# Reordering the head of a fused state-space and gated-MLP kernel: first gate blocks behind two x tiles, weights in fewer and later pieces

## The chip, the cores and the metric

The kernel runs on one core of one Trainium2 chip. The metric is the device time of one execution in microseconds (us); lower is better. The engines are TensorE (PE in the profile, its weight loads PEld), VectorE (DVE), ScalarE (ACT), GpSimd (POOL) and SyncE (SP, which here only issues transfers). Transfers are issued on three queues: SP's, ScalarE's and, for three tiny ones, POOL's.

## The reference

Input x is 2048 tokens of 448 features. It is normalised, goes through a diagonal complex recurrence (448 states) and, beside it, through a gated MLP of width 1792; both are combined:

```python
xn = _layernorm(x, axis=-1)
# A: Lam_bar = exp(dt*Lam);  h_t = Lam_bar*h_{t-1} + B_bar x_t
#    s = 2*Re(C h) + xn*Dskip
s = _A_ref(xn, ...)
# B: g = xn@w_gate; u = xn@w_up; h = sigmoid(g)*u; h@w_down
g = _silu(_B_ref(xn, w_gate, w_up, w_down))
return x + s * g
```

All inputs and the output are bf16.

## The kernel before

The tokens are worked in four chunks of 512 (`NC_`, index c), each of four tiles of 128 tokens (`TPC`). For a chunk the normalised, transposed x stands in `xnT[c % 3]`, in 7 slabs of 64 features, doubled over the two halves of the partitions. The hidden width 1792 is worked in 14 blocks of 128 columns. A *step* `gu_mm(c, k, m, ...)` computes, for k = "g" (gate) or "u" (up), column tile m of both halves of the width: 7 pairs of matmuls (L707, L708), one in each half of the array, into the two banks of a PSUM pair `gu[a]` (three pairs, used in turn by `next_gu`). A gate step is evacuated by ScalarE (Tanh, L721), an up step by VectorE (L724). I write g0.m and u0.m for chunk 0. There are 7 gate and 7 up steps; in chunk 0 the gates come first. Then comes `b_phase` (the state's input matrix), the scans on VectorE, the down projection and the output, chunk by chunk. Two more PSUM banks `acc` serve the transposes and the down projection.

The program is written as operations with costs, reads and writes (`Plan.add`). TensorE runs them in the order written, and while `pl.seq` is set so does VectorE. `Plan.solve` gives each a due time by going back from TensorE's order, then simulates, and each engine's instructions are emitted in the order of the simulated starts. Transfers have a cost of issue and a `rate` in bytes per microsecond that tells the plan when they land; `slot` is the plan's number of a transfer, of which it lets eight be under way at once. The real queues take an eighth-next transfer only when the semaphore that it shares has told of the earlier landing. The rate is a plan's figure only: it can change the order of the instructions, not what a transfer does.

The head, before the first full step, is what the change touches:

- *Loads* (L351 to L412). `load_x` brings tiles of x (112 KB each), `load_w` a block of columns of `w_gate` or `w_up` for one half of the partitions, cut by `BLK`: gate in column tiles (0,2), (2,4), (4,7), 224, 224 and 336 KB a half; up in (0,3), (3,7), 336 and 448 KB a half. SP issues x0, gate half 0 in three, then up in both halves' first blocks, x4 to x7 as one, and up's second blocks, then `dbc`, then the transposing loads of `bT` and all that follows. ScalarE issues x1, x2 and x3 as one, and gate half 1 in three. POOL issues the three rows `vrow`.
- *Norm of tiles 0 to 3*. `stats(t)` (VectorE, L424, L425), `chain(t, 1)` (square root on ScalarE L450, copy on POOL L451, reciprocal on VectorE L452), `norm(t)` (VectorE L469), `pe_transpose(t)` (TensorE L501 to L503), copy to `xnT` (ScalarE for tile 0, L506; VectorE for the others, L509).
- *Columns* (L535). Five tiny matmuls turn `vrow` into columns in a bank of a `gu` pair; VectorE copies them to `pv` (L546); POOL works out `dt`, `theta`, `turn` (L554 to L560), which ScalarE's L575 needs for the tables of sine and cosine.
- *`silu_table`* (L568) loads ScalarE's second table, ahead of all Tanh.

The order of the head stands in L962 to L989: statistics of tiles 0 and 1 and their norms, statistics of tiles 2 and 3, transposes of 0 and 1, columns, norms of 2 and 3, then

```python
    for j in range(2):
        for m in range(2):
            gu_mm(0, "g", m, slots0[m], j, j + 1, not (j or m))
    pe_transpose(2)
    pe_transpose(3)
    silu_table()
    pl.seq = False
    gu_mm(0, "g", 2, slots0[2], 0, 2, True)
    for m in range(3):
        gu_mm(0, "g", m, slots0[m], 2, 4, False)
        gu_evac(0, "g", m, slots0[m])
```

where j counts tiles of 128 tokens: the first blocks are 128 tokens wide, then come four of 256, then g0.3 on with all 512. Tiles 4 to 7 are normed by `stats_for(1)` and `prepare(1)`, ScalarE doing the norm (L474) and SP transposing loads (L375).

## Time and profile before

| what | us |
|---|---|
| runs (median; lowest; highest; three runs) | 185.26; 185.0; 186.19 |
| profiled execution: span from first to last instruction | 183.7 |
| first gate matmul / first matmul of w_up / first of `b_phase` | 7.89 / 19.91 / 30.6 |
| busy: TensorE / VectorE / ScalarE / GpSimd | 177.4 / 166.4 / 94.8 / 34.2 |

Of the profiled execution the record keeps the span and no other time; the span lies 1.6 us under the median of the runs. A line of the timeline has start, busy time, engine, source line, operation, output and inputs, the count and, in brackets, the idle time before it and what ended it. A line of the waits has who waited for whom, the sum, the number of times and the longest. A line of the stretches has each engine's busy time with its number of instructions, then the granted clock, the share of time in which DMA engines were busy (over 1 where packets overlap) and GB/s. The page's rows of digits cut the span into 40 slices, each digit the busy share in tenths.

### The profile page before, as it was taken

To read this page: it belongs to the slowest core of one execution; us is meant where nothing else is said; L and a number is where in the kernel's file an instruction comes from. 1 tells how busy PE (TensorE), PEld (TensorE's weight loads), DVE (VectorE), ACT (ScalarE), POOL (GpSimd) and SP (SyncE) were. 2 spreads that over 40 slices of the span, in tenths; PEclk is the share of its full clock that TensorE was granted. 3 is DMA by queue.
4 is the path that set the end of the run, shared out by engine and by line. 5 is a ranking of instruction groups with operands and counts; after the bars stand their busy time and mean duration, and the time that the engine had idled before them with its cause. 6 is when DMAs were issued, how large, how long until landed. Compare 5 with 4: busy or idle time off the path is not lost.

```text
span 183.7 us, 3601 instructions
## 1 busy us (share of the span) xinstructions
PE 177.4 (97%) x1402; PEld 90.4 (49%) x1402; DVE 166.4 (91%) x296; ACT 94.8 (52%) x152; POOL 34.2 (19%) x95
## 2 busy tenths in 40 slices
PE   7699999999999999999999999999999999999992
PEld 2585555465554444455554444444555444455551
DVE  3873899899999998999999999999999998999973
ACT  3689993958599978665310452367120445211100
POOL 7370465000048557700000000000000000000000
PEclk9999999999999999999999999999999999999999
DMA  5999994489801370243000000002000000001121
GB/s 137 255 225 223 155 166 90 90 256 266 231 0 26 74 82 21 50 82 71 0 2 0 29 0 0 4 0 75 0 4 0 25 25 5 25 0 52 57 73 50
DMA packets 30258, 13.44 MB, mean 73 GB/s; under 512 B 19744, under 2 KB 30240, under 8 KB 30240
## 3 DMA queue, kind: packets, MB, share of 16 engines
q1 hardware_dynamic: 28336, 12.05, 30.7%
q10 hardware_dynamic: 1808, 1.15, 2.5%
q8 instruction: 11, 0.18, 0.4%
q14 instruction: 7, 0.06, 0.1%
q0 software_dynamic: 96, 0.00, 0.0%
HBM read 6.77 MB, written 1.84 MB: 47 GB/s over the span
## 4 chain that ended last, share of the span: by engine, by line
PE 93%; DMA 3%; DVE 1%; issue 1%; POOL 1%; DVEq 0%; POOLq 0%
PE gu L707 45%; PE gu L903 14%; PE acc L932 11%; PE acc L903 9%; PE gu L775 8%; DMA hF<-in_A_Lambda_re_dram 3%; PE gu L708 2%; PE acc L778 2%; PE gu L761 2%; POOL hF L353 1%; PE acc L501 0%; DVE o_t L948 0%; PE acc L764 0%; DVE o_t L944 0%; DVE o_t L941 0%
## 5 line engine op out<-in xcount | busy, mean ns | idle before, releaser
L708 PE MATMUL gu<-xnT,wG 64*128 64x512 bf16 (+2 forms) x245 | 46.0, 333 | 0.0
L707 PE MATMUL gu<-xnT,wG 64*128 64x512 bf16 (+2 forms) x245 | 46.0, 333 | 0.0
L707 PE MATMUL gu<-xnT,wU 64*128 64x512 bf16 x196 | 45.8, 376 | 0.0
L708 PE MATMUL gu<-xnT,wU 64*128 64x512 bf16 x196 | 45.8, 376 | 0.0
L721 ACT ACTIVATE sig<-gu 128x1024 f32<-128x1024 f32 x21 | 21.3, 1021 | 22.0 <-PE gu L708 21.9
L903 PEld LDWEIGHTS <-hF 128*128 128x128 bf16 x224 | 21.9, 98 | 20.7 <-issue 0.2
L707 PEld LDWEIGHTS <-wG 64*128 64x128 bf16 x245 | 21.9, 94 | 18.7
L707 PEld LDWEIGHTS <-wU 64*128 64x128 bf16 x196 | 18.4, 94 | 22.1
L724 DVE SCALAR_TENSOR_TENSOR hF<-sig,gu 128x1024 bf16<-128x1024 f32 x21 | 25.5, 1216 | 2.9 <-PE gu L708 1.6
L903 PE MATMUL gu<-wd,hF 128*128 128x448 bf16 x140 | 27.9, 352 | 0.0
L842 DVE TENSOR_TENSOR_SCAN wv<-c_r,st,z 128x512 bf16<-128x512 f32 x18 | 22.9, 1276 | 0.0
L932 PE MATMUL acc<-cT,hT 128*128 128x448 bf16 (+1 forms) x112 | 22.6, 346 | 0.0
L708 PEld LDWEIGHTS <-wG 64*128 64x128 bf16 x245 | 21.8, 94 | 0.0
L909 ACT ACTIVATE g_t<-gu 128x448 bf16<-128x448 f32 x10 | 5.4, 541 | 29.2 <-DVE o_t L946 12.9
L708 PEld LDWEIGHTS <-wU 64*128 64x128 bf16 x196 | 18.4, 94 | 0.0
L789 ACT CAST bus<-gu 128x1024 bf16<-128x1024 f32 x12 | 11.9, 1011 | 12.4 <-PE gu L761 12.2
L903 PE MATMUL acc<-wd,hF 128*128 128x448 bf16 x84 | 16.9, 352 | 0.0
L775 PE MATMUL gu<-xnT,bT 128*128 128x512 bf16 x72 | 16.7, 379 | 0.0
L932 PEld LDWEIGHTS <-hT 128*128 128x128 bf16 x119 | 11.5, 98 | 10.1 <-issue 0.4
L424 DVE BATCH_NORM_STATS2 bst<-x_all 128x6 f32<-128x448 bf16 x12 | 7.0, 610 | 5.7 <-DMA x_all<-in_A_x_dram 5.7
L795 ACT CAST bus<-acc 64x256 bf16<-64x256 f32 (+1 forms) x24 | 8.8, 369 | 6.4 <-PE acc L778 6.1
L944 DVE TENSOR_TENSOR o_t<-acc,xd 128x448 bf16<-128x448 f32 (+1 forms) x16 | 9.6, 601 | 1.3 <-PE acc L932 1.2
(138 smaller groups left out, 240.1 us busy)
## 6 DMA issues: line engine op xcount, KB each, us to landing
out_dram<-o_t SPq DMA_DIRECT2D x15, 112.0 KB, 1.7
wd<-in_B_w_down_dram SPq DMA_DIRECT2D x2, 784.0 KB, 5.5
x_all<-in_A_x_dram SPq DMA_DIRECT2D x3, 448.0 KB, 4.5
wU<-in_B_w_up_dram SPq DMA_DIRECT2D x2, 448.0 KB, 12.2
wU<-in_B_w_up_dram SPq DMA_DIRECT2D x2, 336.0 KB, 7.6
wG<-in_B_w_gate_dram SPq DMA_DIRECT2D x2, 224.0 KB, 6.5
wG<-in_B_w_gate_dram ACTq DMA_DIRECT2D x2, 224.0 KB, 6.6
xnT<-xn SPq DMA_TRANSPOSE x24, 2.4
```

The lines of the kernel that those rows point to most:

```text
L424: add("DVE", 0.6, lambda: V.bn_stats(out=bst[b][:], in_=x_all[:, t, :]), r=[("x", t)], w=[("bst", b)])
L707: T.matmul(gu[a][:, 0, ts], lhsT=w_[0:H, s, ms], rhs=x[0:H, s, ts], start=(s == 0), stop=(s == 6))
L708: T.matmul(gu[a][:, 1, ts], lhsT=w_[H:P, (s + 1) % 7, ms], rhs=x[H:P, s, ts], start=(s == 0), stop=(s == 6))
L721: add("ACT", act(1024), lambda: A.activation(th, gu[a][:], ACT.Tanh, scale=0.5), r=[("gu", a)], w=[tk])
L724: add("DVE", dve1(1024), lambda: V.scalar_tensor_tensor(out=ho, in0=th, scalar=1.0, in1=gu[a][:], op0=ALU.add, op1=ALU.mult), r=[("gu", a) ...
L775: T.matmul(gu[slots[pt]][:, i, :], lhsT=bT[:, kt, i, pt * P:pt * P + P], rhs=x[:, 2 * kt, :], start=(first and kt == 0), stop=(not first a ...
L789: add("ACT", act(1024), lambda: A.copy(out=bus[u][:], in_=gu[slots[pt]][:]), r=key(pt), w=[("bus", u)])
L795: add("ACT", 0.3, lambda ns=ns, d=d, q=q, l=l, i=i: A.copy(out=bus[u][d, l, ns], in_=acc[a3[i]][q, 0:256]), r=[("acc", a3[i])] + ([("bus", ...
L842: dve(1.194, lambda k=k: V.tensor_tensor_scan(out=wv[:, k, :], data0=rb, data1=z[:, k, :], initial=(st[pt][:, k, :] if c else 0.0), op0=AL ...
L903: T.matmul(d, lhsT=hF[c % 2][:, m, h, js], rhs=wd[:, ft, :], start=(ft == 0), stop=(ft == FT - 1))
L932: T.matmul(y, lhsT=hT[c % 2][:, hm, js], rhs=cT[:, cm, c0:c1], start=(i == 0 and not on_pe), stop=(i == 6))
L944: add("DVE", dve1(n), lambda od=od, y=y, c0=c0, c1=c1: V.tensor_tensor(out=od, in0=y, in1=xq[:, c0:c1], op=ALU.add), r=[key, ("xd", q)], w ...
```

## The change

Loads: x tiles 2 and 3 become two transfers, one on each queue, each behind the first gate block of its queue. x4 to x7 goes ahead of the third gate block on SP. The third gate block of half 1 is issued by ScalarE behind the copy of tile 0's transposes. `w_up` is loaded in one transfer for each half (784 KB): half 0 by SP behind the gate blocks, half 1 by ScalarE, written behind the square root of tile 3. Some rates and slots of the plan differ.

Order: TensorE runs g0.0 and g0.1 on tile 0 and 1, a step at a time, right behind the two tiles' transposes; then tile 2's transposes, g0.2 on tiles 0 and 1, tile 3's transposes, the columns, and then the three steps on tile 2 and on tile 3, 128 tokens at a time. g0.3 has all 512 tokens and goes to the two `acc` banks, from which two Tanh of 512 columns take it. VectorE copies tile 1's transposes before the statistics of tile 2, which with its norm come before those of tile 3; statistics of tile 4 come before tile 3's copy. ScalarE takes over the copy of tile 2's transposes and that of the columns. The columns use an `acc` bank.

In the built program ScalarE's instructions then stand in this order: square roots 0 and 1, copy 0, issue of the third gate block (waits for the landing of half 1's first gate block), square roots 2 and 3, copy 2, table load, columns, issue of `w_up` (waits for the landing of SP's third gate block), Tanh of g0.0, g0.1, g0.2, then Tanh of g0.4, g0.5, g0.6 with norms of tiles 4 to 7 and the four L575 among them, then the Tanh of g0.3. On SP `dbc` and `bT` follow half 0 of `w_up`.

```diff
-    BLK = {"g": [(0, 2), (2, 4), (4, 7)], "u": [(0, 3), (3, 7)]}
+    BLK = {"g": [(0, 2), (2, 4), (4, 7)], "u": [(0, 7)]}
...
     load_x(0, 1, "SP")
+    load_x(1, 1, "ACT")
     load_w("SP", "g", 0, 0, rate=90e3)
-    load_w("SP", "g", 0, 1)
-    load_x(1, 1, "ACT")
-    load_x(2, 2, "ACT")
     load_w("ACT", "g", 1, 0, rate=90e3)
-    load_w("SP", "g", 0, 2)
-    load_w("ACT", "g", 1, 1)
-    load_w("ACT", "g", 1, 2)
+    load_x(2, 1, "SP", rate=300e3)
+    load_x(3, 1, "ACT", rate=300e3)
+    load_w("SP", "g", 0, 1, rate=165e3)
+    load_w("ACT", "g", 1, 1, rate=165e3)
+    load_x(4, 4, rate=230e3)
+    load_w("SP", "g", 0, 2, rate=150e3)
...
-    for h in range(2):
-        load_w("SP", "u", h, 0, rate=215e3)
-    load_x(4, 4, rate=140e3)
-    for h in range(2):
-        load_w("SP", "u", h, 1, rate=260e3)
+    load_w("SP", "u", 0, 0, rate=150e3, slot=10)
...
-        add("DVE", 0.6, lambda: V.bn_stats(out=bst[b][:], in_=x_all[:, t, :]), r=[("x", t)], w=[("bst", b)])
+        add("DVE", 0.6, lambda: V.bn_stats(out=bst[b][:], in_=x_all[:, t, :]),
+            r=[("x", t)] + ([("xnT", 0, 3, "a")] if 4 < t < 8 else []), w=[("bst", b)])
...
-        if t == 0:
+        if t in (0, 2):
             add("ACT", 0.85, lambda: A.copy(out=xnT[0][:, :, js], in_=tp[:, :, :]),
...
-        vps = flat(gu[a][:, 0, 0:12], 4, 3)
+        vps = flat(acc[a][:, 0:12], 4, 3)
...
-        add("DVE", 0.1, lambda: V.tensor_copy(out=pv[:].rearrange("p k i -> p i k"), in_=vps[:]), r=[("gu", a)], w=["pv"])
+        add("ACT", 0.2, lambda: A.copy(out=pv[:].rearrange("p k i -> p i k"), in_=vps[:]), r=[("acc", a)], w=["pv"])
...
+        if a is None:
+            for i in range(2):
+                add("ACT", act(512), lambda i=i: A.activation(th[:, i, :], acc[i][:], ACT.Tanh, scale=0.5),
+                    r=[("acc", i)], w=[tk] if i == 0 else [(tk, 1)])
...
-    stats(2)
-    stats(3)
     slots0 = [next_gu() for _ in range(3)]
     pe_transpose(0)
+    load_w("ACT", "g", 1, 2, rate=150e3, r=[("xnT", 0, 0, "a")], slot=11)
     pe_transpose(1)
-    columns(slots0[2])
-    for t in (2, 3):
-        chain(t, 1)
-        norm(t)
-    for j in range(2):
-        for m in range(2):
+    stats(2)
+    chain(2, 1)
+    norm(2)
+    stats(3)
+    chain(3, 1)
+    load_w("ACT", "u", 1, 0, rate=150e3, r=[("sd", 3)], slot=13)
+    norm(3)
+    for m in range(2):
+        for j in range(2):
             gu_mm(0, "g", m, slots0[m], j, j + 1, not (j or m))
     pe_transpose(2)
+    stats(4)
+    for j in range(2):
+        gu_mm(0, "g", 2, slots0[2], j, j + 1, not j)
     pe_transpose(3)
+    columns(0)
     silu_table()
     pl.seq = False
-    gu_mm(0, "g", 2, slots0[2], 0, 2, True)
-    for m in range(3):
-        gu_mm(0, "g", m, slots0[m], 2, 4, False)
-        gu_evac(0, "g", m, slots0[m])
+    for j in range(2, 4):
+        for m in range(3):
+            gu_mm(0, "g", m, slots0[m], j, j + 1, False)
+            if j == 3:
+                gu_evac(0, "g", m, slots0[m])
+    gu_mm(0, "g", 3, None, 0, TPC, False)
+    gu_evac(0, "g", 3, None)
...
-    for i in range(3, 13):
+    for i in range(4, 13):
         gu_step(0, i)
```

More of the change, by code (lines that the diff above doesn't have):

```diff
@@ L358, in load_x, with load_w @@
              x_all[:, t0:t0 + n, :], x_src[:, t0:t0 + n, :], r=r, rate=rate)
-    BLK = {"g": [(0, 2), (2, 4), (4, 7)], "u": [(0, 3), (3, 7)]}
-    def load_w(eng, k, half, b, r=(), rate=105e3):
+    BLK = {"g": [(0, 2), (2, 4), (4, 7)], "u": [(0, 7)]}
+    def load_w(eng, k, half, b, r=(), rate=105e3, slot=None):
         m0, m1 = BLK[k][b]
@@ L368, in load_w @@
              wsrc[k][:, c0 + m0 * P:c0 + m1 * P].rearrange("(s p) f -> p s f", p=H), cost=0.65, r=r, rate=rate)
+        if slot is not None:
+            pl.ops[-1].slot = slot
     def load_wd(h):
@@ L542, in f @@
                 T.matmul(vps[h * H:h * H + H, 3, :], lhsT=vrow[:, 384:448], rhs=ident[0:3, 0:3], start=True, stop=True)
-        add("PE", 0.4, f, r=["ident"] + [("vrow", k) for k in range(3)], w=[("gu", a)])
+        add("PE", 0.4, f, r=["ident"] + [("vrow", k) for k in range(3)], w=[("acc", a)])
         pv = sbt("pv", [3, 4], FP32)
         dt_b = C("dt", 4, BF16)
-        add("DVE", 0.1, lambda: V.tensor_copy(out=pv[:].rearrange("p k i -> p i k"), in_=vps[:]), r=[("gu", a)], w=["pv"])
+        add("ACT", 0.2, lambda: A.copy(out=pv[:].rearrange("p k i -> p i k"), in_=vps[:]), r=[("acc", a)], w=["pv"])
         dt_b = C("dt", 4, BF16)
@@ L567, in silu_table @@
     def silu_table():
-        add("ACT", 1.3, lambda: A.preload_act_table_set("silu_and_others"), r=[("sd", t) for t in range(4)], w=["silutab"])
+        add("ACT", 1.3, lambda: A.preload_act_table_set("silu_and_others"), r=[("sd", t) for t in range(4)] + [("xnT", 0, 2, "a")], w=["silutab"])
     def tables():
@@ L700, in gu_mm @@
         x = xnT[c % 3]
+        bank, keys = ([gu[a][:, 0, :], gu[a][:, 1, :]], [("gu", a)]) if a is not None else (
+            [acc[0][:], acc[1][:]], [("acc", 0), ("acc", 1)])
         ts = slice(lo * P, hi * P)
@@ L706, in f @@
             for s in range(7):
-                T.matmul(gu[a][:, 0, ts], lhsT=w_[0:H, s, ms], rhs=x[0:H, s, ts], start=(s == 0), stop=(s == 6))
-                T.matmul(gu[a][:, 1, ts], lhsT=w_[H:P, (s + 1) % 7, ms], rhs=x[H:P, s, ts],
+                T.matmul(bank[0][:, ts], lhsT=w_[0:H, s, ms], rhs=x[0:H, s, ts], start=(s == 0), stop=(s == 6))
+                T.matmul(bank[1][:, ts], lhsT=w_[H:P, (s + 1) % 7, ms], rhs=x[H:P, s, ts],
                          start=(s == 0), stop=(s == 6))
@@ L711, in gu_mm @@
         return add("PE", 7 * (0.0028 + n / 2400.0) + (2 * SW if first else 0), f,
-                   r=xr(c, lo, hi) + [("w", k, 0, m), ("w", k, 1, m)], w=[("gu", a)], name=f"{k}{c}.{m}")
+                   r=xr(c, lo, hi) + [("w", k, 0, m), ("w", k, 1, m)], w=keys, name=f"{k}{c}.{m}")
     sg_n = [0]
@@ L719, in gu_evac @@
         ho, hk = hF[c % 2][:, m, :, :], ("hF", c % 2, m)
-        if k == "g":
+        if a is None:
+            for i in range(2):
+                add("ACT", act(512), lambda i=i: A.activation(th[:, i, :], acc[i][:], ACT.Tanh, scale=0.5),
+                    r=[("acc", i)], w=[tk] if i == 0 else [(tk, 1)])
+        elif k == "g":
             add("ACT", act(1024), lambda: A.activation(th, gu[a][:], ACT.Tanh, scale=0.5),
@@ L725, in gu_evac @@
                                                                  op0=ALU.add, op1=ALU.mult),
-                r=[("gu", a), tk], w=[hk])
+                r=[("gu", a), tk] + ([(tk, 1)] if (tk, 1) in pl.w else []), w=[hk])
     def gu_step(c, i, first=False):
@@ L993, in stats_for @@
             if c not in (3,):
-                stats(t)
+                if t != 4:
+                    stats(t)
             elif t % 2:
```

## The prediction

> **What bounds the kernel now.** I read the page first: share of TensorE, then its row over the 40 slices; after that the timelines of the head and the loads.
>
> ```profile
> PE 177.4 (97%) x1402; PEld 90.4 (49%) x1402; DVE 166.4 (91%) x296; ACT 94.8 (52%) x152; POOL 34.2 (19%) x95
> PE   7699999999999999999999999999999999999992
> PEclk9999999999999999999999999999999999999999
> ```
>
> TensorE is busy in every slice but the first two and the last, at full clock, so the kernel is one unbroken row of matmuls between a head and a tail. Nothing after the head has slack: what the head gains or loses reaches the end unchanged. A later stall is not made up either. So the question is only: at what moment does the gapless row stand at a fixed point of it, say the first up matmul, before and after? I call that matmul u0.0.
>
> The timeline of TensorE from 5 to 20 us, cut to the rows where its work changes:
>
> ```profile
> 5.34 0.51 PE L501 MATMUL acc<-ident,xn 128*128 128x128 bf16 x6 [0.49 <-DVE xn L469]
> ...
> 7.63 0.21 PE L540 MATMUL gu<-ident,hF 3*128 3x3 bf16 x3 [0.99 <-DMA hF<-in_A_Lambda_re_dram]
> 7.89 0.23 PE L707 MATMUL gu<-xnT,wG 64*128 64x128 bf16 x1
> 9.56 0.51 PE L501 MATMUL acc<-ident,xn 128*128 128x128 bf16 x6
> 10.79 0.28 PE L707 MATMUL gu<-xnT,wG 64*128 64x256 bf16 x1
> 13.87 0.38 PE L707 MATMUL gu<-xnT,wG 64*128 64x512 bf16 x1
> 19.91 0.38 PE L707 MATMUL gu<-xnT,wU 64*128 64x512 bf16 x1
> ```
>
> The columns wait for the last of three tiny loads (0.99 us), and the first gate block stands behind them. The starts give prices: columns 0.26 us; four 128-column blocks with their lead-in 1.55 (0.39 each); a tile's transposes 0.62; eight 128-columns' worth at width 256 3.08; four full steps 6.04, so 1.51 each. From 7.63 to 19.91 there is no gap.
>
> The timeline of VectorE shows what a tile's norm costs:
>
> ```profile
> 5.46 0.40 DVE L469 TENSOR_SCALAR xn<-x_all,meanf,rsd 128x448 bf16<-128x448 bf16 x1
> 5.78 0.62 DVE L424 BATCH_NORM_STATS2 bst<-x_all 128x6 f32<-128x448 bf16 x1
> 6.43 0.18 DVE L425 BATCH_NORM_AGGREGATE mv<-bst 128x2 bf16<-128x6 f32 x1
> ...
> 7.26 0.59 DVE L509 COPY xnT<-acc 128x896 bf16<-128x896 bf16 x1
> ...
> 8.35 0.40 DVE L469 TENSOR_SCALAR xn<-x_all,meanf,rsd 128x448 bf16<-128x448 bf16 x1
> 8.92 0.40 DVE L469 TENSOR_SCALAR xn<-x_all,meanf,rsd 128x448 bf16<-128x448 bf16 x1
> ```
>
> Statistics of tiles 2 and 3 fill the pause in which VectorE would wait for the transposes of tile 1; both tiles are normed by 9.32, before TensorE asks at 9.56. That cover is what the change gives up.
>
> Last the loads: the view of the tile wU, and three stretches (5 to 11, 12 to 19, 19 to 22 us; last columns clock, DMA share, GB/s).
>
> ```profile
> L353 SPq DMA_DIRECT2D wU<-in_B_w_up_dram x4: 595/616/630, 7.1 to 9.8; - x4
> DMA to landing us min/median/max: 7.1/9.9/12.7
> 5.00:11.00 6.00, 4.67 (x97) 3.81 (x99) 4.49 (x15) 3.70 (x7) 2.69 (x11) 1.00 1.10 248
> 12.00:19.00 7.00, 7.00 (x86) 4.61 (x84) 3.37 (x8) 7.00 (x10) 1.34 (x4) 1.00 1.12 222
> 19.00:22.00 3.00, 3.00 (x31) 1.60 (x28) 2.88 (x11) 3.00 (x7) 1.18 (x3) 1.00 1.38 129
> ```
>
> The DMA engines are full until 20 us: 248 GB/s while both queues have work, 222 with SP's alone. The last part of wU lands at 9.8 + 12.7 = 22.5. Today that harms nobody: u0.0 needs only the first three column tiles of wU (336 KB a half, issued at 7.1 and 7.7, median 7.6 us to landing, so by about 16), and step 3, which needs the rest, starts at 19.91 + 3 x 1.51 = 24.4.
>
> **The change, part by part.**
>
> *Start of the first block.* It stands behind the copy of tile 0 alone (6.07 to 6.98) and its weights. x0, x1 and both first gate blocks are 672 KB, moved by about 5.0 us at the rates shown; landing follows the last byte by about 1. So it starts at 7.03 instead of 7.89: 0.86 earlier, of which 0.26 goes back where the columns now stand.
>
> *Tiles 2 and 3.* VectorE now copies tile 1 first (transposes done 6.64, copy from 6.70; such copies follow each other by 0.55) and starts tile 2's statistics at 7.25 instead of 5.78. From statistics to norm: 0.65 + 0.22 + 0.44 + 0.26 = 1.57 (rows of tile 1), norm 0.40, transposes 0.05 later: tile 2's transposes at 9.26. Tile 3's statistics follow that norm by 0.32, at 9.13; its transposes start at 9.13 + 2.02 = 11.15, against 10.18 now. TensorE has 1.55 us of work from 7.03 and idles from 8.58 to 9.26, then 0.62 + 0.78 and idles from 10.66 to 11.15.
>
> *From there to u0.0.* 11.15 + 0.62 + 0.26 (columns) + 2.33 (six 128-column blocks) + 6.04 = 20.40. Width 128 in place of 256 costs 0.002 a pair, nothing. So TensorE alone reaches u0.0 0.49 later than now.
>
> *Statistics of tile 4 ahead of the copy of tile 3.* They wait for x4..7, whose bytes (896 KB of x, 896 KB of gate blocks, part of the late one) were moved by 9.3 to 10.8 us in the run before; with 0.7 to 1.5 to landing (an estimate: ScalarE's last gate block landed at 3.15 + 9.1 = 12.2, and its bytes with all ahead of them had been moved by about 11) that is 10 to 12.3. The copy is needed at 13.16, so landing up to 11.7 is free: 0 to 0.6, taken as 0, since the wait for wU below covers it.
>
> *ScalarE.* It takes over one transposed copy (0.91) and the copy of the columns (about 0.2), both free there. Two issues of loads now stand in its stream, 0.6 to 0.7 each (rows of its queue). The second, for wU, stands ahead of all Tanh and waits, by its semaphore, for the landing of SP's last gate block. That has 2464 KB ahead of and in it; that many were moved by 12.3, landing 13.4 to 14.8. ScalarE would be there at 12.65 (table load 1.28 after tile 2's copy, then columns). Behind it queue all Tanh; the first must end by 15.87 for step 4, and would end at 14.7, or at 16.4 with the longest wait: at most 0.5, inside the wait below. The four L575 (0.63 each), hidden today at 10.04 to 12.56 in a wait, come among Tanh (0.92) and norms (0.65), because the columns come 4.5 us later; POOL's 1.86 us from columns to turn is hidden by three Tanh. Sum with no wait: 13.75 + 6 x 0.92 + 4 x 0.63 + 3 x 0.65 = 23.7 for the Tanh that frees the third accumulator pair, needed by the third up step at 20.40 + 3.02 = 23.4. That is 0.4 late, or up to 1.7 with the wait; nothing if u0.0 is as late as below.
>
> *Step 3 in the accumulators.* Two Tanh of 512 columns in place of one of 1024, about 0.1 more; they come after step 6's and are needed only when step 3's up block is evacuated, at 26.4, and the banks only at 30.8. Nothing.
>
> *wU in one piece.* This is the term that decides. u0.0 now needs both whole halves, that is every byte of x0..7, wG and wU, 4032 KB, the same bytes that landed last at 22.5. Between 20.4 and 22.5 TensorE has nothing else in its order. Corrections: two queues run for longer (248 for 222 GB/s from about 14 on, or all along: 0.6 to 1.2 earlier, 0.9 taken); dbc (112 KB) is on SP's ring behind its half and shares the engines with ScalarE's late half: 0.5 later; the transposing loads of bT behind dbc may share the last microsecond: 0 to 1.3, 0 taken as they come last. 22.5 - 0.9 + 0.5 = 22.1. Ends: 20.4 (packets of 1792 B instead of 768 and 1024 run as the 512 B ones did at 5 us, 297 GB/s) and 23.9.
>
> A rule speaks to this place. The Trainium skill, "DMA: Bandwidth & Descriptors", Rules for kernel authors, says that transfers to the two partition halves serialize on the same 16 engines and that issuing from more queues does not add bandwidth; by it the 0.9 goes and u0.0 stands at 23.0. Its section Bandwidth gives 341 GB/s for a 1 MB load; by that (an estimate from that page) 1568 KB of wU would take 4.7 us and land near 19, so no wait. The rows here show neither: 248 against 222 with two queues, and no gain of 448 KB loads over 336 KB ones.
>
> *POOL and SP.* POOL's three column loads are unmoved; its statistics for tiles 4..7 come about 8 us earlier, in idle time. SP issues bT behind dbc as before. No cost, since bT is needed only at 30.8.
>
> **Sum.** u0.0 at 22.15 against 19.91: 2.2 us later, and TensorE behind it is the same row of work. The profiled span is 183.7 us, 185.9 after. The median of the runs is 185.26, 1.6 above that span (start and end around it); I add the same: 187.5 us. About 1%, 1.85 us, is what a measurement of this kernel can tell from no change.
>
> **The rivals.**
> - *Weights in time* (30 in 100). wU lands by 21.3 or sooner; then the chain of tile 3 (+0.49) and the Tanh queue (+0.4 more) set the time: +0.5 to +1.4, about 186.1. For it: 297 GB/s at 5 us with both halves in flight. Against: 217 to 240 ever after.
> - *A gain* (8 in 100). If tiles 2 and 3 come in time for a gapless row from 7.03 and wU lands by 19.2, the 0.86 less the columns' 0.26 remain: u0.0 at 19.3, 184.6 us. It decides at tile 3's transposes starting by 10.0. Against: VectorE's order, which puts copy, statistics and norm of two tiles one after another.
> - *Later still* (12 in 100). bT's transposes share the engines with the last of wU, as at 19 to 22 us where the rate fell to 129: landing past 23.5, +3.6 to +5, about 189.5.
>
> **How the numbers follow.** The forecast (u0.0 from 21.3 to 23.5, +1.4 to +3.6) gets 50 in 100. Range: forecast and weights in time together, 80 in 100: 185.7 to 189.0; the forecast alone 186.6 to 188.9. Slower by over 1%: four fifths of the forecast, 40, and all of the last rival, 12: 52. Faster by over 1%: 2, as the whole gain is under 1%. Within 1%: 46.
>
> **What would show it.** Right: first gate matmul near 7.0; idle TensorE of about 0.7 and 0.5 before the transposes of tiles 2 and 3; a wait of 1 to 3 us at the first wU matmul, ended by a load of wU; ScalarE's issue of wU past 13. Wrong: no wait there, wU landed by 20.4, or a gap later in the row that I have not named.

## The result and the profile after

The changed kernel takes 193.09 us (median of four runs, 192.90 to 193.22) against 185.26 (four runs too, 185.00 to 186.19): 1.0397 times as long, 95% interval [1.0339, 1.0456]. Medians, here and below, count every execution; the ratios leave out those more than 1.5% above the fastest of their kernel. The forecast was 187.5, the range 185.7 to 189.0. The profiled execution took 192.9, its span is 191.1, so 7.4 us of span are to be found.

The page of the kernel after, the lines that answer to those of before, and one of its queues:

```profile
PE 181.4 (95%) x1458; PEld 91.9 (48%) x1458; DVE 166.4 (87%) x294; ACT 95.5 (50%) x155; POOL 35.7 (19%) x95
...
PE   7893999999899999999999999999999999999992
...
PEclk9999699999999999999999999999999999999999
...
q8 instruction: 11, 0.18, 0.4%
```

The row of matmuls now has a hole in its fourth slice (14.3 to 19.1 us) and a lower clock in the fifth. There are 56 matmuls and 56 weight loads more (the blocks of 128 tokens).

The timeline of TensorE, kernel after, rows where its work changes:

```profile
5.38 0.82 PE L501 MATMUL acc<-ident,xn 128*128 128x128 bf16 x6
7.45 0.21 PE L709 MATMUL gu<-xnT,wG 64*128 64x128 bf16 x1 [0.27 <-ACT xnT L506]
9.71 0.51 PE L501 MATMUL acc<-ident,xn 128*128 128x128 bf16 x6 [0.46 <-DVE xn L469]
11.50 0.51 PE L501 MATMUL acc<-ident,xn 128*128 128x128 bf16 x6 [0.21 <-DVE xn L469]
14.75 0.38 PE L709 MATMUL acc<-xnT,wG 64*128 64x512 bf16 x1
...
15.39 0.38 PE L709 MATMUL acc<-xnT,wG 64*128 64x512 bf16 x1
19.07 0.39 PE L710 MATMUL acc<-xnT,wG 64*128 64x512 bf16 x1 [3.30 <-issue]
...
20.42 0.63 PE L710 MATMUL gu<-xnT,wG 64*128 64x512 bf16 x1
...
25.95 0.38 PE L709 MATMUL gu<-xnT,wU 64*128 64x512 bf16 x1
26.42 0.39 PE L710 MATMUL gu<-xnT,wU 64*128 64x512 bf16 x1
```

g0.3 starts at 14.75 (before 13.87: +0.88). In its middle TensorE stands for 3.30 us and waits for no engine and no load: the releaser is "issue". From 20.3 to 23.7 a matmul of 512 columns takes 0.63 instead of 0.38: the granted clock is 0.50 there (last of the stretches below). The second half of w_up, landed at 26.4, lets its first matmul start at 26.42. So 19.91 has become 26.42, 6.5 us, made up of 0.88, 3.46 (19.07 less 15.39, less the 0.22 from one pair of matmuls to the next), 1.70 (half of 3.41 us at half clock), and 0.47 (26.42 less 25.95). The last 0.9 come later: 0.53 in one wait of TensorE for ScalarE at 51.67, the rest in pieces too small to place.

VectorE, kernel after:

```profile
7.23 0.62 DVE L509 COPY xnT<-acc 128x896 bf16<-128x896 bf16 x1 [1.33 <-PE acc L503]
7.78 0.63 DVE L423 BATCH_NORM_STATS2 bst<-x_all 128x6 f32<-128x448 bf16 x1
9.26 0.40 DVE L469 TENSOR_SCALAR xn<-x_all,meanf,rsd 128x448 bf16<-128x448 bf16 x1
11.04 0.40 DVE L469 TENSOR_SCALAR xn<-x_all,meanf,rsd 128x448 bf16<-128x448 bf16 x1
11.64 0.63 DVE L423 BATCH_NORM_STATS2 bst<-x_all 128x6 f32<-128x448 bf16 x1 [0.20 <-DMA x_all<-in_A_x_dram]
```

The chain of tiles 2 and 3 runs as forecast, 0.4 later throughout. The loads: the tile wU, then the stretches 5 to 11, 12 to 19, 19 to 22 and 20.4 to 23.7 us, kernel after.

```profile
L353 SPq DMA_DIRECT2D wU<-in_B_w_up_dram x1: 633/633/633, 7.5 to 7.5; - x1
L353 ACTq DMA_DIRECT2D wU<-in_B_w_up_dram x1: 603/603/603, 14.8 to 14.8; - x1
...
DMA to landing us min/median/max: 11.6/11.8/12.0
```
```profile
5.00:11.00 6.00, 5.28 (x107) 4.21 (x107) 3.60 (x11) 1.86 (x5) 0.39 (x3) 1.00 1.16 244
12.00:19.00 7.00, 3.77 (x99) 2.93 (x98) 3.26 (x11) 4.57 (x7) 3.60 (x9) 1.00 1.20 183
19.00:22.00 3.00, 2.93 (x20) 1.22 (x22) 2.30 (x7) 1.15 (x2) 2.07 (x6) 0.72 1.05 244
20.40:23.70 3.30, 3.30 (x18) 1.24 (x16) 1.84 (x4) 0.90 (x1) 0.67 (x1) 0.50 1.10 237
```

SP's half landed at 7.5 + 12.0 = 19.5, ScalarE's at 14.8 + 11.6 = 26.4. The view of the transfers from 15.5 to 20.0 us, and then from 20.0 to 24.2 us (q1 is SP's queue, q10 ScalarE's, q8 TensorE's instructions):

```profile
q1 hardware_dynamic: 1518, 0.69, 116.7%
q8 instruction: 1, 0.02, 1.9%
```
```profile
q10 hardware_dynamic: 464, 0.80, 90.7%
q1 hardware_dynamic: 736, 0.17, 20.8%
```

ScalarE issued its 0.80 MB at 14.8, and not a packet of it moved before 20.0; what moved was SP's: the rest of its half, dbc and transposing loads of bT, issued from 9.8 on.

So there are two theories. A: TensorE runs out of instructions. They come in packets of 16 KB (q8, which moved 11 of them while TensorE worked 1458 matmuls and 1458 weight loads, so one for about 265), and the packet is late. B: ScalarE's half of w_up stands behind what SP issued before 14.8. Both end near 26.4, so each hides the other.

### The profile page after: what moved, and what is told of

Its sections match the earlier page's. It is cut to its first block, busy times and chain, and to the rows that moved or that the text cites. A ratio compares the mean times of both kernels' runs of the same rounds, so it can differ in the third digit from the quotient of the medians.

```text
span 191.1 us, 3713 instructions
## 1 busy us (share of the span) xinstructions
PE 181.4 (95%) x1458; PEld 91.9 (48%) x1458; DVE 166.4 (87%) x294; ACT 95.5 (50%) x155; POOL 35.7 (19%) x95
## 4 chain that ended last, share of the span: by engine, by line
PE 78%; issue 5%; SPq 5%; ACT 5%; DMA 3%; DVE 3%; POOL 1%; DVEq 0%; ACTq 0%; POOLq 0%
PE gu L709 31%; PE gu L909 14%; PE acc L938 11%; PE acc L909 8%; PE gu L781 5%; SPq L377 4%; DMA xnT<-in_A_C_im_dram 3%; PE gu L710 3%; PE gu L417 2%; ACT hF L727 2%; PE acc L501 1%; ACT ctmp L673 1%; PE gu L767 1%; ACT xn L474 1%; PE acc L784 1%
## 5 line engine op out<-in xcount | busy, mean ns | idle before, releaser
L709 PE MATMUL gu<-xnT,wG 64*128 64x512 bf16 (+2 forms) x266 | 46.6, 322 | 0.3 <-ACT xnT L506 0.3
L710 PE MATMUL gu<-xnT,wG 64*128 64x512 bf16 (+2 forms) x266 | 46.6, 322 | 0.0
L709 PEld LDWEIGHTS <-wG 64*128 64x128 bf16 x273 | 22.8, 96 | 15.6
L909 PE MATMUL gu<-wd,hF 128*128 128x448 bf16 x140 | 27.9, 352 | 0.0
L710 PEld LDWEIGHTS <-wG 64*128 64x128 bf16 x273 | 22.7, 96 | 8.0 <-issue 6.3
L938 PE MATMUL acc<-cT,hT 128*128 128x448 bf16 (+1 forms) x112 | 22.6, 346 | 0.0
L915 ACT ACTIVATE g_t<-gu 128x448 bf16<-128x448 f32 x10 | 5.4, 539 | 29.2 <-DVE o_t L952 12.9
L781 PEld LDWEIGHTS <-bT 128*128 128x128 bf16 x72 | 7.0, 98 | 7.5
## 6 DMA issues: line engine op xcount, KB each, us to landing
wU<-in_B_w_up_dram ACTq DMA_DIRECT2D x1, 784.0 KB, 11.6
```

What stands on the lines that cost most here:

```text
L709: T.matmul(bank[0][:, ts], lhsT=w_[0:H, s, ms], rhs=x[0:H, s, ts], start=(s == 0), stop=(s == 6))
L710: T.matmul(bank[1][:, ts], lhsT=w_[H:P, (s + 1) % 7, ms], rhs=x[H:P, s, ts], start=(s == 0), stop=(s == 6))
L781: T.matmul(gu[slots[pt]][:, i, :], lhsT=bT[:, kt, i, pt * P:pt * P + P], rhs=x[:, 2 * kt, :], start=(first and kt == 0), stop=(not first a ...
L909: T.matmul(d, lhsT=hF[c % 2][:, m, h, js], rhs=wd[:, ft, :], start=(ft == 0), stop=(ft == FT - 1))
L938: T.matmul(y, lhsT=hT[c % 2][:, hm, js], rhs=cT[:, cm, c0:c1], start=(i == 0 and not on_pe), stop=(i == 6))
```

## The experiments

Medians; the ratio is to the kernel before on the same chip, with its interval. "w_up" is the matmul from which w_up's steps run on, "half clock" the time at half clock between the first full clock and the end, both from the profiled execution; other executions of the same run can have more or less of it. Runs 13 to 18 ask what twelve left open: why ScalarE's half is late, and what the rest of the change costs.

| run | us | ratio | w_up | half clock |
|---|---|---|---|---|
| kernel before | 185.26 | | 19.91 | 0 |
| kernel after | 193.09 | 1.0397 [1.0339, 1.0456] | 26.42 | 3.41 |
| 1 before, narrow blocks | 188.09 | 1.0133 [1.0063, 1.0202] | 23.90 | 0 |
| 2 after, wide blocks | 193.45 | 1.0415 [1.0343, 1.0487] | 25.54 | 6.83 |
| 3 after, both halves on SP | 191.48 | 1.0302 [1.0236, 1.0368] | 25.38 | 3.41 |
| 4 both (2 and 3) | 190.00 | 1.0206 [1.0124, 1.0287] | 23.58 | 0 |
| 5 wide, bT held back in the plan | 191.39 | 1.0264 [1.0204, 1.0325] | 25.79 | 3.41 |
| 6 wide, w_up in four | 192.19 | 1.0329 [1.0282, 1.0377] | 26.87 | 10.24 |
| 7 as 6, statistics 4 later | 192.13 | 1.0325 [1.0269, 1.0380] | 26.76 | 6.83 |
| 8 before, columns late, x2, x3 early | 186.53 | 1.0045 [1.0017, 1.0073] | 19.85 | 0 |
| 9 wide, bT loaded plainly | 195.81 | | 27.72 | 3.41 |
| 10 as 6, other order | 192.95 | 1.0360 [1.0282, 1.0438] | 27.52 | 10.24 |
| 11 as 7, other order | 192.66 | 1.0352 [1.0275, 1.0429] | 27.29 | 6.83 |
| 12 as 1, w_up not loaded | 186.90 | 1.0058 [0.9999, 1.0117] | | 0 |
| 13 wide, bT behind ScalarE's half | 192.60 | 1.0400 [1.0362, 1.0438] | 25.15 | 3.41 |
| 14 wide, w_up in four, all on SP | 188.00 | 1.0158 [1.0116, 1.0199] | 22.69 | 0 |
| 15 as 14, statistics 4 later | 188.35 | 1.0151 [1.0114, 1.0187] | 21.62 | 0 |
| 16 before, columns behind first blocks | 185.38 | 1.0010 [0.9980, 1.0040] | 19.85 | 0 |
| 17 before, one piece a half | 189.46 | 1.0168 [1.0087, 1.0249] | 22.64 | 3.41 |
| 18 as 13, statistics 4 later | 193.11 | 1.0367 [1.0249, 1.0486] | 24.01 | 0 |

### A: TensorE's instructions (runs 1, 2 and 12)

Run 1, kernel before:

```diff
-    gu_mm(0, "g", 2, slots0[2], 0, 2, True)
+    for j in range(2):
+        gu_mm(0, "g", 2, slots0[2], j, j + 1, not j)
     for m in range(3):
-        gu_mm(0, "g", m, slots0[m], 2, 4, False)
+        for j in range(2, 4):
+            gu_mm(0, "g", m, slots0[m], j, j + 1, False)
```


> The kernel before with one edit: the first block of g0.2 and the second blocks of g0.0, g0.1, g0.2 are cut from 256 tokens to 128 (56 pairs of matmuls instead of 28, same columns; 112 more TensorE instructions with their weight loads by 14 us). Loads, ScalarE and VectorE are as before. Theory A (TensorE runs out of stored instructions when it issues many in a short time while the DMA engines are full): in the changed kernel it stops after about 450 of its instructions; here it has issued 450 at about 15.0 us instead of 20.8, and the 16 KB of the instruction queue that started at 14.99 in the run before must land first; so an idle TensorE of 1 to 3 us near 15 us, ended by nothing that the profile shows, 186.3 to 188.5 us. Rival C (the idle stretch at 15.39 us of the changed kernel belongs to step g0.3 in the accumulator banks, or to the changed loads): no idle stretch, 185.3 us.

Run 2, kernel after:

```diff
-    for j in range(2, 4):
-        for m in range(3):
-            gu_mm(0, "g", m, slots0[m], j, j + 1, False)
-            if j == 3:
-                gu_evac(0, "g", m, slots0[m])
+    for m in range(3):
+        gu_mm(0, "g", m, slots0[m], 2, 4, False)
+        gu_evac(0, "g", m, slots0[m])
```


> The changed kernel with the second blocks of g0.0 to g0.2 put back to 256 tokens (42 pairs of matmuls fewer become 21: 84 TensorE instructions fewer before g0.3). Theory A: the stored instructions last until about 19.5 us, the next ones have landed by then, so the idle 3.3 us at 15.39 go. Theory B (ScalarE's half of wU lands at 26.4, whatever TensorE does): u0.0 still starts at 26.4, now after 4 to 6 us of idle there, which halves the clock behind it: 192.5 to 194.5 us. If A alone carried the loss: u0.0 at 21, 187 us. Rival C: idle stretch at 15.4 stays, 193 us.

Run 12, run 1 with, in `gu_mm`, `w_ = wgt["g"]` and:

```diff
-    for h in range(2):
-        load_w("SP", "u", h, 0, rate=215e3)
     load_x(4, 4, rate=140e3)
-    for h in range(2):
-        load_w("SP", "u", h, 1, rate=260e3)
```


> The first run (kernel before with the later blocks of g0.0 to g0.2 cut to 128 tokens, stall of 3.4 us in g0.3, instruction packet at 15.55 us) without the loads of w_up: the up steps of all chunks read w_gate instead, so w_up is left out and SP has 1568 KB less between x4..7 and bT. Theory A (the next 16 KB of TensorE's instructions come through the same DMA engines and are late because those are full of weights until 20 us): the instruction packet starts 1.5 us earlier or more, the stall falls under 2 us or goes. Rival A2 (the packet is asked for and served at a time that does not depend on the other transfers): packet at 15 to 16 us and a stall of 3 us or more, as in the first run.

Timelines of TensorE, run 1, then run 12; the packet of instructions in the view of the transfers of run 1 from 15.5 to 16.0 us and of run 12 from 13.2 to 14.0; and the stretch 0 to 15.6 us of the kernel after (the numbers of matmuls and of weight loads stand in the first two brackets):

```profile
18.71 0.39 PE L708 MATMUL gu<-xnT,wG 64*128 64x512 bf16 x1 [3.37 <-issue]
```
```profile
15.86 0.39 PE L704 MATMUL gu<-xnT,wG 64*128 64x512 bf16 x1 [1.37 <-issue]
```
```profile
q8 instruction: 1, 0.02, 19.4%
```
```profile
q8 instruction: 1, 0.02, 8.6%
```
```profile
0.00:15.60 15.60, 13.49 (x223) 9.00 (x223) 9.17 (x27) 5.79 (x10) 6.01 (x23) 1.00 0.93 197
```

The narrow blocks alone make the hole in the kernel before (3.37 us, above the 1 to 3 expected; time +2.7, as expected), and the wide ones take it out of the kernel after. TensorE stopped at the same count in every profile with this hole, the kernel after and runs 1, 3 and 12: 223 matmuls and 223 weight loads had started. It went on 1.4 to 1.6 us behind the end of the packet's transfer (kernel after: packet from 16.27 to 17.67, next matmul at 19.07). In the kernel before it has started 346 when the packet begins (14.99 us), and the packet comes in time. With w_up not loaded the packet starts 2.2 us earlier (13.31 for 15.55), the hole shrinks to 1.37, and the span is 1.1 us above that of the kernel before instead of 4.2. A holds: more and shorter instructions use up the supply sooner, and with 1568 KB more to move the next 16 KB come later. What exactly gives the packet its turn stays open: it started between 13.3 and 18.7 us in the runs, when 298 to 446 matmuls and weight loads had begun.

In run 2 TensorE is at w_up at 21.09 and then waits for ScalarE's half (timeline of TensorE, run 2):

```profile
25.54 0.60 PE L710 MATMUL gu<-xnT,wU 64*128 64x512 bf16 x1 [4.08 <-DMA wU<-in_B_w_up_dram]
```

Nothing is won, as expected (192.5 to 194.5): B alone ends at 25.5.

### B: ScalarE's half of w_up (runs 3, 4, 5, 9, 13 and 18)

Run 3, kernel after; run 4 is the same with run 2's edit:

```diff
     load_w("SP", "u", 0, 0, rate=150e3, slot=10)
+    load_w("SP", "u", 1, 0, rate=215e3, slot=11)
...
-    load_w("ACT", "u", 1, 0, rate=150e3, r=[("sd", 3)], slot=13)
```


> The changed kernel, with half 1 of wU issued by SP right behind half 0 instead of by ScalarE behind the columns. Theory B: wU lands whole by 21.5 to 23. Theory A: the idle 3.3 us in g0.3 and the half clock behind it stay, so u0.0 starts at 24 to 26: 190.5 to 192.5 us. If B alone carried the loss: u0.0 at 22.3, 187.7 us.

> Both edits: blocks of 256 tokens and half 1 of wU on SP behind half 0. A and B together: no idle in g0.3, u0.0 at 21.5 to 22.8 by the landing of wU: 187.0 to 188.3 us. If a third cause carried part of the loss, it stays above 189.5.

In run 3 w_up is there at 22.5, and TensorE comes at 25.4 only, because of its hole: 1.6 us won, all as expected. Both edits together win 3.1. Neither theory alone explains the loss, and the two together explain less than half of its 7.8: run 4 missed its expectation by 1.7 and fell to the case named beside it, a third cause. Its timelines say why; TensorE, then VectorE:

```profile
14.33 0.27 PE L710 MATMUL gu<-xnT,wG 64*128 64x256 bf16 x1 [1.43 <-DVE xnT L510]
23.58 0.39 PE L711 MATMUL gu<-xnT,wU 64*128 64x512 bf16 x1 [0.54 <-DMA wU<-in_B_w_up_dram]
```
```profile
12.92 0.63 DVE L424 BATCH_NORM_STATS2 bst<-x_all 128x6 f32<-128x448 bf16 x1 [1.04 <-DMA x_all<-in_A_x_dram]
```

Statistics 4 wait for x4..7 with tile 3's copy behind them, and one piece a half is late even on SP.

Run 5, run 2 with:

```diff
-            tload([("bT", i)], bT[:, 0:3, i, :], m[:, 0:384], D * 768)
+            tload([("bT", i)], bT[:, 0:3, i, :], m[:, 0:384], D * 768, r=[("w", "u", 1, 6)])
```


> The wide blocks of the second run (193.45 us; no stall in g0.3, but ScalarE's half of wU issued at about 15 and landed at 25.5, first packets near 20) with SP's transposing loads of bT held back until ScalarE's half of wU has landed. Theory B1 (SP's transposing loads, in issue from 9.8 to 19.1 us, hold up ScalarE's transfer): the packets of ScalarE's half start within 1 to 2 us of its issue, it lands at 20 to 22, u0.0 stands at 21 to 22 and the time is 187 to 188.5. Rival B2 (the engines are simply full with other bytes, or one queue's 784 KB is slow by itself): landing past 24 as before, time 191.5 or more.

The edit is one of the plan alone, and in the built program SP's order and waits were those of run 2, so this run tells neither theory. It is a repeat of run 2 with ScalarE's issue ahead of its copy of the columns; the half landed at 25.7 again. It was 2.1 us faster than run 2; 1.7 of that is the clock, as far as the two profiles show (3.41 us at half clock for 6.83), and the rest was not followed up.

Run 9, run 2 with plain loads for bT (`D * 256` likewise):

```diff
-            tload([("bT", i)], bT[:, 0:3, i, :], m[:, 0:384], D * 768)
+            load("SP", ("bT", i), D * 768, bT[:, 0:3, i, :], m[0:384, :].rearrange("(k p) f -> p k f", p=P))
```


> The wide blocks of the second run, with the four transposing loads of bT replaced by plain loads of as many bytes (the transposition of B is left out, 896 B rows; SP's other instructions stay). Theory B1 (SP's transposing loads, in issue for up to 9.3 us together, hold up ScalarE's half of wU): its packets start within 1 to 2 us of its issue at about 15, it lands at 19 to 22 instead of 25.5, u0.0 stands at 21 to 22.5, and the time is 188.0 to 190.5 (0.4 to 1.5 us of waits for x4..7 stay). Rival B2 (784 KB on ScalarE's queue is late because the engines are full with SP's bytes): landing at 24 or later, 192 or more.

The tile wU, run 9:

```profile
L353 ACTq DMA_DIRECT2D wU<-in_B_w_up_dram x1: 602/602/602, 15.5 to 15.5; - x1
...
DMA to landing us min/median/max: 12.2/12.7/13.1
```

SP was done issuing bT at 14.0, and the half landed later still, at 27.7. So the long issue of the transposing loads (theory B1) is not needed to make the half late: their bytes, issued earlier, were moved first. It has a part all the same. In the kernel after, the transfer engines were nearly idle from 18.4 to 19.2 us (share 0.15, 26 GB/s), while ScalarE's half, issued at 14.8, had not moved a packet:

```profile
18.40:19.20 0.80, 0.13 (x2) 0.11 (x4) 0.00 (x0) 0.80 (x2) 0.20 (x1) 1.00 0.15 26
```

Run 13, run 2 with, behind ScalarE's issue of w_up:

```diff
+    add("ACT", 0.25, lambda: A.copy(out=bT[0:1, 0, 0, 0:1], in_=pio2[0:1, :]), r=["pio2"], w=[("bT", 0)], chain=True)
```


> The wide blocks of the second run; between ScalarE's issue of its half of wU and SP's first transposing load of bT stands a copy of one element by ScalarE into bT, which that load overwrites, so SP issues all loads of bT behind ScalarE's half (at about 15.5 us). Theory B3 (the engines work off what was issued earlier first, across queues; bT's first transposing loads, issued from 9.8 us on, stood ahead of ScalarE's half): the half's packets follow right on those of SP's half and dbc, it lands at 20.5 to 22.5 instead of 25.5, u0.0 at 21 to 22.6, 188.5 to 190.5 (a wait for x4..7 stays). Rival B4 (784 KB on ScalarE's queue is late because that queue is served last while SP's has work, whenever it was issued, or is slow by itself): 25 again, 192 or more.

Run 18 is run 13 with `stats(4)` moved behind `pe_transpose(3)`.

> The thirteenth run with the statistics of tile 4 behind tile 3's copy. If the wait for x4..7 (1.8 us idle, then 3.4 us at half clock) set its time, that goes, TensorE reaches u0.0 by 21.5 and waits there for ScalarE's half of wU: landing at 23.5 to 25 by theory B3 with its bytes counted (784 KB behind SP's half at about 205 GB/s are 3.9 us, which the thirteenth run's expectation left out), 189.5 to 191. If wU's half on ScalarE is late whatever else is moved: 192 or more again, with the landing at 25.5 or later.

The tile wU, run 18:

```profile
L353 ACTq DMA_DIRECT2D wU<-in_B_w_up_dram x1: 603/603/603, 10.6 to 10.6; - x1
...
DMA to landing us min/median/max: 12.9/13.1/13.4
```

In both, SP's bT stood behind ScalarE's half, and the half landed ahead of bT: 25.1 in run 13 (bT's first load 25.9), 24.0 in run 18. By the terms set for run 13 its rival B4 came out ("25 again, 192 or more"). But in both runs ScalarE's issue also came 3 us earlier than in run 2 (11.3 and 10.6 for 14.1), and all loads of run 13 ran late (x4..7 landed at 13.7, in run 2 at 11.0). Counted from the landing of SP's half, ScalarE's came 6.8 to 6.9 us later where bT stood ahead (kernel after, runs 2 and 9; 5.6 in run 5) and 3.7 and 3.3 where it stood behind (runs 13 and 18). There its packets began at 17, when about four fifths of SP's half had been moved, so the two halves overlapped.

Against B4 speaks the kernel after itself. ScalarE issued its third gate block at 6.5, SP its own at 6.8 and its half of w_up at 7.5, and from 10 to 11 us it was ScalarE's queue that moved while SP's stood:

```profile
q10 hardware_dynamic: 225, 0.17, 108.3%
q1 hardware_dynamic: 15, 0.01, 6.8%
```

The order by time of issue (B3) fits all of these records. My landing of 20.5 to 22.5 was wrong by the 3.9 us that 784 KB need at 205 GB/s; counted, as for run 18, it comes out (23.5 to 25). The time did not follow, and both expectations of it were missed: in run 13 TensorE stood 1.80 us for the late x4..7, half clock followed, and it reached w_up at 25.15, just behind the landing (25.08); in run 18 it waited 2.25 for w_up, and then four times (0.79, 0.58, 0.40, 0.36) for VectorE and ScalarE. So the order of the transfers is shown, but not that curing it alone wins time.

### The rest of the change (runs 6, 7, 10, 11, 14, 15 and 17)

Runs 6 and 10, run 2 with `BLK["u"] = [(0, 3), (3, 7)]` and all four pieces of w_up on SP, in run 10 written behind ScalarE's third gate block; in runs 7 and 11 also `stats(4)` behind `pe_transpose(3)`.

> Wide blocks, and w_up in the four pieces of the kernel before (336 and 448 KB a half), all issued by SP behind the gate blocks, transposing loads of bT behind them. What is left of the change is the new order of the x tiles and statistics. Theory (one piece for each half makes u0.0 wait for bytes that only step 3 needs): no wait on wU at u0.0 and no stall in g0.3; against the 190.0 us of the fourth run (one piece a half, both on SP) 0.5 to 1 us is gained by that, with the wait for x4..7 (about 1.4 in that run) left: 187.5 to 189.5. Rival (what is left over 187 in the fourth run has nothing to do with the pieces): 190 again.

> The run with w_up in four pieces, and the statistics of tile 4 behind tile 3's copy in place of ahead of it. Theory (VectorE, waiting for x4..7, keeps tile 3's copy from TensorE): the idle time of TensorE that ends with a VectorE copy goes (0.4 to 1.4 us), the time is 186.0 to 187.3, which is the 0.5 us that tile 3's later transposes cost, and little else. Rival (x4..7 is not what the copy waits for): within 0.2 us of the run beside it.

> What the sixth run was meant to be: wide blocks, w_up in the four pieces of the kernel before, all on SP behind the gate blocks, but emitted behind ScalarE's third gate block, so that this one does not wait for the landing of SP's second gate block (that wait, 3.8 us on ScalarE ahead of tile 2's square root, spoiled the sixth and seventh runs). Theory (one piece a half makes u0.0 wait): no wait on wU at u0.0; what is left is tile 2's and 3's later transposes (0.5) and the wait of statistics 4 for x4..7 (0.4 to 1.5): 186.3 to 188.5. Rival (the rest over 187 in the fourth run has another source): 190.

> The same with the statistics of tile 4 behind tile 3's copy. Theory: TensorE's idle time that ends with a VectorE copy of xnT goes, u0.0 at 20.2 to 20.8, 185.7 to 186.8, so nearly all of the change's loss is undone with its order of the first blocks kept. Rival: no difference to the run beside it, over 0.2 us.

All four missed, for one reason that the edit brought in. ScalarE and TensorE, timelines of run 10:

```profile
10.77 0.60 ACTq L353 DMA_DIRECT2D wG<-in_B_w_gate_dram  x1
11.42 0.30 ACT L448 ACTIVATE sdb<-mv,epsc 128x1 bf16<-128x1 bf16 x1 [4.42 <-DMA wG<-in_B_w_gate_dram]
```
```profile
12.47 0.82 PE L499 MATMUL acc<-ident,xn 128*128 128x128 bf16 x6 [3.17 <-DVE xn L467]
```

More transfers ahead gave ScalarE's third gate block another shared semaphore, that of SP's second gate block, which landed at 10.75. ScalarE waited for it with tile 2's square root behind, TensorE stood 2.6 to 3.2 us, and the clock was half for 6.8 to 10.2 us. The block itself landed at 21.5 to 22.9 (13.0 in the kernel after), behind the pieces of w_up that SP had issued meanwhile, and three gate steps that read it, 4.5 us, stand ahead of w_up: that puts w_up at 26 to 27.4. In runs 7 and 11 TensorE waited 1.0 for it; in runs 6 and 10 the half clock lasted until 21.0 and 21.6, and TensorE came 0.9 and 0.1 behind its landing. One execution of run 6 had no half clock (mean granted clock 1.00) and took 191.95, hardly less than the others (192.16 to 192.35). These runs tell nothing of the pieces, but much of a late issue on a busy engine. In runs 14 and 15, with run 2's edit and the four pieces, ScalarE issues nothing late:

```diff
     load_w("SP", "g", 0, 2, rate=150e3)
+    load_w("SP", "g", 1, 2, rate=150e3)
...
-    load_w("SP", "u", 0, 0, rate=150e3, slot=10)
+    for b in range(2):
+        for h in range(2):
+            load_w("SP", "u", h, b, rate=215e3)
...
-    load_w("ACT", "g", 1, 2, rate=150e3, r=[("xnT", 0, 0, "a")], slot=11)
...
-    load_w("ACT", "u", 1, 0, rate=150e3, r=[("sd", 3)], slot=13)
```


> Wide blocks; the third gate blocks of both halves and then w_up in the four pieces of the kernel before, all issued by SP; ScalarE issues nothing after 3 us. Of the change there remain the order of the first blocks and of tiles 2 and 3, the columns behind tile 3, step 3 in the accumulators and statistics 4 ahead of tile 3's copy. Theory (one piece a half costs u0.0 its wait, which was 0.5 us in the fourth run, and statistics 4 cost up to 1.4): tile 2's transposes at 9.7 to 10.2, no wait on wU, 186.5 to 189. Rival (the rest over 187 of the fourth run has another source): 190.

> The run beside it with the statistics of tile 4 behind tile 3's copy. Theory: the idle time of TensorE that ends with VectorE's copy of tile 3 goes; u0.0 at 20.2 to 20.9; 185.7 to 187, 0.4 to 1.5 below the run beside it, and close to the kernel before with the 0.5 of tile 3's chain left. Rival: within 0.2 us of the run beside it.

Run 14's time came as expected, with no wait on w_up, though tile 2's transposes stood at 10.67 and not at 9.7 to 10.2. Its median is 2.0 us under run 4, but the intervals of the two ratios overlap, and the third gate block of half 1 moved to SP with the pieces, so this pair alone does not price the pieces; run 17 does, on the kernel before. Run 15 missed its expectation (185.7 to 187): it is no faster, so the place of statistics 4 costs nothing that the times show. The profiled execution of run 14 was its slowest (189.73), and its wait of 0.94 us for tile 3's copy need not be typical. What is left of the change in run 15, timelines of TensorE:

```profile
10.10 0.51 PE L504 MATMUL acc<-ident,xn 128*128 128x128 bf16 x6 [1.05 <-DVE xn L472]
11.88 0.51 PE L504 MATMUL acc<-ident,xn 128*128 128x128 bf16 x6 [0.21 <-DVE xn L472]
```
```profile
52.68 1.67 PE L912 MATMUL gu<-wd,hF 128*128 128x448 bf16 x8 [1.04 <-ACT bus L798]
```

Tile 3's transposes 1.7 later than before, so w_up 1.7 later; and 1.0 where ScalarE is late with a copy that TensorE needs (because its Tanh and tables were put together, as I take it; no run shows that). Both together are the 2.8 us of its span, to 0.1.

Run 17, kernel before with `BLK["u"] = [(0, 7)]` and:

```diff
-    for h in range(2):
-        load_w("SP", "u", h, 0, rate=215e3)
     load_x(4, 4, rate=140e3)
     for h in range(2):
-        load_w("SP", "u", h, 1, rate=260e3)
+        load_w("SP", "u", h, 0, rate=215e3)
```


> The kernel before with w_up in one transfer of 784 KB for each half, both on SP, behind x4..7; nothing else of the change. Theory (the deciding term of the prediction: u0.0 then waits for the last byte of w_up, which landed at 22.5 in the kernel before and at 22.5 to 23.5 in the runs with both halves on SP): TensorE waits 2.5 to 3.5 us at its first wU matmul at 19.9, u0.0 at 22.4 to 23.4, 187.8 to 188.8; 1.7 more if the clock halves behind the wait, as it did behind waits of 2.6 us and more. Rival (big pieces move faster and land by 20.5): 185.2 to 186.

TensorE, run 17, and its stretch 23 to 27 us (clock in the third number from the end):

```profile
22.64 0.39 PE L706 MATMUL gu<-xnT,wU 64*128 64x512 bf16 x1 [2.72 <-DMA wU<-in_B_w_up_dram]
```
```profile
23.00:27.00 4.00, 4.00 (x26) 1.50 (x22) 2.67 (x6) 3.97 (x9) 2.31 (x10) 0.57 1.39 184
```

This is the deciding term of the prediction by itself: w_up landed at 22.6 (22.1 forecast), u0.0 2.7 later, and 1.7 more by the clock, all as expected. The four executions say the same of the clock: the one without half clock (mean granted clock 1.00) took 187.87, the others, at 0.99, 189.45 to 190.02.

### Two parts alone on the kernel before (runs 8 and 16)

Run 8: `columns(0)` in an accumulator bank behind `pe_transpose(3)`, and x2, x3 one on each queue ahead of the gate blocks. Run 16, the kernel before with:

```diff
     pe_transpose(1)
-    columns(slots0[2])
...
             gu_mm(0, "g", m, slots0[m], j, j + 1, not (j or m))
+    columns(slots0[2])
     pe_transpose(2)
```


> The kernel before with two parts of the change alone: the columns behind tile 3 in an accumulator bank, and x2 and x3 one on each queue ahead of the gate blocks. Blocks, statistics' order and w_up's pieces stay as before. If the 0.99 us wait for the tiny column loads is all that stood ahead of the first gate block, it starts about 0.6 earlier and the whole row moves by that: 184.7 us. Rival (tile 2 and 3 cannot keep up, the time won at the start is idle time ahead of their transposes): 185.2 to 185.5. A loss, 186 or more, if the gate blocks, now behind x2 and x3, land too late.

> The kernel before with one thing moved: the columns stand behind the first four 128-token gate blocks instead of ahead of them (same bank, VectorE's copy of them behind the norms of tiles 2 and 3). The first block then waits for ScalarE's first gate block alone (landed 7.5 in the run before): start 7.55 for 7.89, tile 2's transposes 9.2 for 9.56, u0.0 0.3 earlier: 184.9 us. Rival (columns later by 1.5 us make the sine tables and with them the Tanh queue late, as in the eighth run): 185.3 to 186.5.

Both start the first gate block earlier (7.09 and 7.42 for 7.89) and reach w_up at 19.85, hardly earlier than before (19.91). Run 16 came out at its rival (185.38), run 8 at its third case, a loss (186.53). In run 16 the columns take 0.28 of the 0.47 back ahead of tile 2 (9.37 for 9.56), the rest goes in pieces too small to place. In run 8 the second half of the first gate block lands 0.3 late, then the columns wait for the copy of tile 2 that frees their bank; behind w_up TensorE waits 0.36 and 0.32 us for VectorE at 27.9 and 31.8 (for late evacuations; why they are late is not shown), and the run is 0.8 slower than the kernel before beside it (185.75). No version that beats the kernel before came out.

## Why the prediction was wrong, point by point

Two steps failed, both terms put at nothing. The first is "Width 128 in place of 256 costs 0.002 a pair, nothing": it cost 3.46 us of missing instructions and 1.70 of clock. The second is "0 taken as they come last" for the transposing loads of bT: they came first, and the second half of w_up landed at 26.4 instead of 22.1. The direction was right, but not its mechanism: of the signs named, the wait of 1 to 3 us at the first matmul of w_up did not show (25.95, its second half 26.42), and the gap "that I have not named" did.

- *Start of the first block* (7.03): 7.45. The transposes of tile 0 ran at half clock (0.82 for 0.51), so all behind is 0.4 later. The step held but for that.
- *Tiles 2 and 3* (9.26, 11.15; idle 0.67, 0.49): 9.71, 11.50; 0.46, 0.21. Held, with the same 0.4. (The four blocks with their lead-in, taken as 1.55, are 1.67 by the starts shown, 7.89 to 9.56, so the first idle time should have been 0.56.)
- *From there to u0.0* (TensorE alone 20.40): 25.95. This step failed first. In matmul time the 0.002 a pair is right. The 112 more instructions of the blocks made TensorE run dry after 446, in the kernel before as well (run 1), and the hole was followed by half clock.
- *Statistics of tile 4* ("taken as 0"): 0.20 of wait here, TensorE not held up. Held; in run 4 it was 1.43, by a landing at 12.9.
- *ScalarE* (issue past 13): 14.8, held. The Tanh queue "0.4 late" did not hold TensorE at the third up step; its one wait of that size for ScalarE is 0.53 at 51.67.
- *wU in one piece* (22.1): 22.6 in run 17, 22.5 in run 3 and 23.5 in run 4, so the term was near for two halves on SP. In the kernel after it was 26.4, by the second failed step: ScalarE's issue waited until 14.8, and bT's first load was issued at 9.8. The rival *later still* (past 23.5) had that place, with 12 in 100 and 189.5 us.
- *Sum*: a wait of 2 us was priced at 2 us. Behind run 17's wait of 2.7 the clock took 1.7 more. The work behind u0.0 was not quite the same row either: 0.9 us came later, 0.53 of it at 51.67.
- The rule weighed there (the Trainium skill, "DMA: Bandwidth & Descriptors", Rules for kernel authors: more queues add no bandwidth) was not put to the test: the two halves were not moved side by side (from 15.5 to 20.0 us SP's queue alone, then ScalarE's 0.80 MB), so my 0.9 for two queues had no occasion. Both halves on SP were faster (191.48 for 193.09) by their order. The estimate from that page's 341 GB/s, a landing near 19, did not show: 22.5.

## What to carry to other kernels

Count the instructions that an edit adds to an engine's row, not only their time: here the next packet of them came later the more weights there were to move, and a row of short matmuls ran dry. In these runs a transfer's place in line was set by when it was issued, so an issue that waits on a busy engine puts its bytes behind everything that others issued meanwhile, and holds up the engine's own work behind it. A hole of two to three us in TensorE's row can cost 1.7 us more by the clock, and is to be priced with it.
